# Attention followed by a gated mixture of experts: reordering the preparation of the leftover expert at the end of the kernel

## The chip, the core and the metric

The kernel runs on one core of a Trainium2 chip. The metric is the device time of one execution in microseconds; the median of three runs before the change is 463.12 us (463.02 to 463.18). All other times come from one execution taken by the hardware profiler, whose span from the first to the last instruction is 462.4 us; its mean granted TensorE clock is 0.997 of full speed.

## What is computed

Multi-query attention (8 batches, 16 heads, 384 tokens, head size 64, one key and value head per batch) gives `x` with 3072 rows of 1024. Each row then goes through one of 16 experts (4 groups of 4), chosen by two argmax gates and weighted by both softmax values:

```python
attn = softmax(q @ k.T / 8) @ v              # per batch and head
x = attn.transpose(0, 2, 1, 3).reshape(3072, 1024)
g_idx = argmax(x @ w_group)                  # 4 groups
e_idx = argmax(x @ w_expert[g_idx])          # 4 experts in the group
out[tok] = g_w * e_w * (relu(x[tok] @ w1[g, e]) @ w2[g, e])
```

With these inputs nearly all rows of a batch choose the same expert. So the kernel computes, for each batch, the one most frequent expert over all its 384 rows, with a weight of zero for rows that chose another. What is left over is handled apart: the kernel keeps a table of the (batch, expert) pairs that are also needed. One such pair is computed on the fast path for up to 32 tokens ("the leftover pair"); if more pairs or more tokens turn up, or the scores are too large for an exponential without a maximum, a branch ("the rare case") at the end does the work slowly. In this draw the branch is not taken.

## The kernel before

**Stages.** A loop over 24 steps (8 batches of 3 blocks of 128 tokens) computes scores, exponentials and values for attention; beside it the expert work runs in *units*. The unit list of a batch has 14 entries: 8 "h" units (line 407: eight 128x384 matmuls into one PSUM buffer, evicted by ScalarE on line 408) and 6 "y" units (line 417: eight 128x512 matmuls, evicted on line 419, or by `merge` on line 449, and stored on lines 439 and 441). Numbers like y(1,0) below mean block of tokens 1, left half of the columns. `fill(n)` (line 476) emits the next n units of whichever batch comes next. There is no scheduler: each engine's order is the order of the program, written out by hand, and `fill` is what puts TensorE work between the short, dependent steps of the other engines.

**The end.** After the loop only units remain, and the leftover pair has to be found, gathered, computed and added. Before the change the order from line 639 on is:

1. three y units of batch 6, then the last values of attention (`values`, `join`, `invert`, `weigh`). `weigh` makes `xbf`, the bf16 input of the experts, and stores it to `x_bf` in DRAM (line 303).
2. two y units, the gate matmuls of the last two blocks (line 312), the gate's softmax on VectorE (`gate_math`), `bound_a`, then two units (the last y of batch 6 and h0 of batch 7), `counts(None, last)` (line 340, PE; line 342, ACT; then six VectorE operations of `gate_c`) and `bound_b` (line 512, two transposes, then four VectorE operations), which tests whether the scores were small enough.
3. the load of `xe` (line 656): all rows of the batch that holds the leftover pair, read back from `x_bf`. Its batch number is a register, so it must wait for the store of line 303. Then a chain of short VectorE operations from `gi` (line 659) to `mb` (line 667).
4. one unit (h1), the prefix counts `pr` (lines 672 and 673), eight VectorE operations to `pick`, the 0/1 matrix which sends token to slot; two units (h2, h3), `pg` (line 691), the transpose of `of_last` (line 698), and VectorE operations up to `rarei`, the flag of the rare case (line 710).
5. one unit (h4); then three times eight transposes `pb` of `xe` (line 717) with one unit after each (h5, h6, h7); the gather `px` (line 726), y(0,0), the hidden layer `ph` (735), y(0,1), its transpose `phT` (741), y(1,0), the output `py` (749), y(1,1), `spread`.
6. `spread` (line 453) turns the leftover rows that belong to the last 128 tokens of the output into a tile `yl`: eight matmul records on line 458 and two ScalarE copies on line 461. The leftover rows elsewhere are scattered to DRAM by one indirect DMA on GpSimd (line 755). y(2,0), then the register load of `rarei` on all five engines (line 757), then y(2,1) in two parts of 256 columns; all three are evicted by `merge`, which adds `yl`.
7. the branch on `rare` (line 809; the profile puts its instructions on line 810), and the end of the kernel (line 901).

**Buffers.** `side` tiles (`hps`, `yps`, `pr`, `pg`, `pb` ...) share three PSUM buffers in rotation, so a PE step waits for the reader of the tile three allocations before. `ps_m` has one more buffer. **Queues.** The DMA issues of SyncE (lines 303, 439, 441, 656) run in program order, and one that waits holds those behind it. Leftover `w1` and `w2` are loaded by GpSimd (lines 145, 574); `w2` starts when the last y unit of batch 6 has freed its buffer.

Of the kernel before, what the change touches and what calls it, by code (L numbers as in the profile page):

```python
# [9 lines left out]
FP32 = mybir.dt.float32  # L10
BF16 = mybir.dt.bfloat16
I32 = mybir.dt.int32
U32 = mybir.dt.uint32
P = 128
ACTF = mybir.ActivationFunctionType
OP = mybir.AluOpType
AX = mybir.AxisListType.X
# [4 lines left out]
def kernel(  # L22
# [406 lines left out]
    def first_units(b):  # L429
        rows = {}  # L430

        def place(st, cs):
            if cs.start == 0:
                rows[st] = pool.tile([P, Dm], FP32, tag="y", bufs=3, name="y")
            return rows[st][:, cs]

        def store(st, cs, y):
            if closes(st):
                nc.sync.dma_start(out=outv[b, :, st, cs], in_=y)
            elif cs.stop == Dm:  # L440
                nc.sync.dma_start(out=outv[b, :, st, :], in_=rows[st][:])

        def closes(st):
            return b == B - 1 and st == ST - 1

        def merge(st, cs, ps, y):
            if not closes(st):
                return False
            nc.vector.scalar_tensor_tensor(out=y, in0=ps[:], scalar=gsel[b][:, st:st + 1], in1=leftover["y"][:, cs], op0=OP.mult, op1=OP.add)
            return True  # L450
        return moe_units(wts[b][0], wts[b][1], xbf[b], lambda: gsel[b], place, store, merge, lambda st, nh: 2 if closes(st) and nh == 1 else 1)

    def spread():
        lo = [ps_m.tile([P, 2, CW], FP32, tag="o", name="lo"), side([P, 2, CW], FP32, "lo2")]
        for i in range(2):
            for c in (i, 2 + i):
                r = slice(CAP * c, CAP * c + CAP)
                nc.tensor.matmul(out=lo[c // 2][:, c % 2, 0:QW], lhsT=leftover["spread"][r, :], rhs=leftover["yc"][r, :], start=True, stop=True, tile_position=(CAP * c, 0))
        t = pool.tile([P, Dm], FP32, tag="pt", bufs=9, name="yl")
        for i in range(2):  # L460
            nc.scalar.copy(out=t[:, i * CW:(i + 1) * CW].rearrange("p (c n) -> p c n", c=2), in_=lo[i][:, :, 0:QW])
        leftover["y"] = t

    NP = B * ST
# [11 lines left out]
    def fill(n):  # L476
        while n > 0:
# [10 lines left out]
            if ran[0] == (FO + 2 * ST) * (B - 1):  # L488
                leftover_w2()

    def gates(b):
        if b == 0:
            choose_a(0, gate_a(0, 0, 1))
            return
        ps = gate_a(b, 0, ST)
        choose_a(b, ps)
        gate_logits(b - 1, ps, 1, ST)
        gate_math(b - 1)
# [76 lines left out]
        leftover["w2"] = w2  # L575
    for p in range(NP):
        b, st = divmod(p, ST)
        jobs = [lambda: gates(0), lambda: None, lambda: counts(0, None)] if p == 2 else []
        if p == 0 or p == ST or (st == 1 and 1 < b < B - 1):
            load_q(b + 1)  # L580
        for j in range(3):
            scores(p, j)
            if p == 0 and j == 0:
                turn_q(1, lambda h: q_raw[0][:, 1, h], [nc.vector.tensor_copy])
        if p == 0:
            stats_k(0)
            prep_k(1)
        elif p == ST:
            prep_q(p + 1)
        if jobs:  # L590
            jobs.pop(0)()
        for j in (1, 2):
            pre_add(p, j)
        for j in range(KB):
            if p > 0:
                values(p - 1, j)
            if j == 2 and p > 0:
                join(p - 1)
            if j + 3 < KB:
                scores(p, j + 3)  # L600
            if 0 < j < 4:
                pre_add(p, j + 2)
            if j == 2 and p > 0:
                invert(p - 1)
            if j == 3:
                stats_q(p)
                if p == 1:
                    turn_q(2, lambda h: q_raw[0][:, 2, h], [nc.scalar.copy])
                elif p == 2:
                    turn_q(3, lambda h: q_nat[0][:, h], [nc.scalar.copy])  # L610
            if jobs:
                jobs.pop(0)()
            if p == ST + 1 and j == 0:
                fill(3)
            if st == 1 and 0 < b < B - 1 and j == 0:
                load_k(b + 1)
            if 0 < j < 5:
                some_q(1 if p <= ST + 1 else 2)
            if st == 1 and b + 1 < B and j == KB - 1:
                load_v(b + 1)  # L620
        assert not jobs
        if p > 0:
            weigh(p - 1)
        fold_keys(p)
        if st == 2 and b + 1 < B:
            stats_k(b + 1)
        if p in PHASES:
            n = PHASES[p]
            steps = {}
            prep_q(p + 1)  # L630
            if b == B - 1:
                steps = {1: lambda: gates(b), 2: lambda: counts(b, None), 3: lambda: (counts(None, b - 1), early_pair())}
            else:
                steps = {2: lambda: gates(b), 4: lambda: (counts(b, b - 1), turns(p))}
            for i in range(n):
                fill(1)
                if i in steps:
                    steps[i]()
    fill(3)
    for j in range(KB):  # L640
        if j == 2:
            join(NP - 1)
# [1 line left out]
    invert(NP - 1)  # L644
    weigh(NP - 1)
    last = B - 1
    fill(2)
    gate_logits(last, gate_a(last, 1, ST), 1, ST)
    gate_math(last)
    bound_a()  # L650
    fill(2)
    counts(None, last)
    bound_b()

    xe = pool.tile([P, KO, S], BF16, tag="qraw", bufs=2, name="xe")
    nc.sync.dma_start(out=xe[:].rearrange("p k s -> p (k s)"), in_=xb_dram[bass.ds(leftover["b"], 1)].rearrange("a p k -> (a p) k"))
    gi = leftover["gi"]
    ge = gi[:, :, 0]
    nc.vector.tensor_copy(out=ge, in_=gate_all[:, bass.ds(leftover["reg"], 1), :].rearrange("p a s -> p (a s)"))
# [5 lines left out]
    nc.vector.tensor_copy(out=mb[:, 1, 1:2], in_=m[:, 0:1])  # L665
    nc.vector.tensor_add(out=mb[:, 1, 2:3], in0=m[:, 0:1], in1=m[:, 1:2])
    nc.vector.tensor_add(out=mb[:, 1, 3:4], in0=mb[:, 1, 2:3], in1=m[:, 2:3])
    nfl = pool.tile([P, 1], FP32, tag="nfl", bufs=1, name="nfl")
    nc.vector.reduce_sum(out=nfl[:], in_=extra[:], axis=AX)
    fill(1)  # L670
    pr = side([P, CW], FP32, "pr")
    nc.tensor.matmul(out=pr[:, 0:4], lhsT=prefix[:], rhs=mb[:, 0, :], start=True, stop=False)
    nc.tensor.matmul(out=pr[:, 0:4], lhsT=ones_bf[:], rhs=mb[:, 1, :], start=False, stop=True)
    rk = pool.tile([P, 4], FP32, tag="rk", bufs=1, name="rk")
    nc.vector.tensor_copy(out=rk[:], in_=pr[:, 0:4])

    small = pool.tile([P, 2], FP32, tag="small", bufs=1, name="small")
    nc.vector.tensor_scalar(out=small[:, 0:1], in0=leftover["known"][:], scalar1=1.0, scalar2=None, op0=OP.is_ge)
    nc.vector.scalar_tensor_tensor(out=small[:, 0:1], in0=rk[:, 3:4], scalar=float(CAP), in1=small[:, 0:1], op0=OP.is_le, op1=OP.mult)
# [1 line left out]
    pick = pool.tile([P, ST, P], FP32, tag="part", bufs=1, name="pick")  # L681
    for st in range(ST):
        nc.vector.tensor_scalar(out=pick[:, st, :], in0=rank_of[:], scalar1=rk[:, st:st + 1], scalar2=m[:, st:st + 1], op0=OP.is_equal, op1=OP.mult)
    pick_bf = pool.tile([P, ST, CAP], BF16, tag="kT", name="pick_bf")
    nc.vector.tensor_copy(out=pick_bf[:], in_=pick[:, :, 0:CAP])
    of_last = pool.tile([P, 2, P], FP32, tag="presum", bufs=1, name="of_last")
    nc.vector.tensor_scalar(out=of_last[:, 0, :], in0=pick[:, ST - 1, :], scalar1=leftover["final"][:, 0:1], scalar2=None, op0=OP.mult)
    fill(2)
    pg = side([P, CW], FP32, "pg")
    for st in range(ST):  # L690
        nc.tensor.matmul(out=pg[:, 0:2], lhsT=pick[:, st, :], rhs=gi[:, st, :], start=(st == 0), stop=(st == ST - 1))
    gc = pool.tile([P, 2], FP32, tag="gc", bufs=1, name="gc")
    nc.vector.tensor_copy(out=gc[:, 0:1], in_=pg[:, 0:1])
    nc.vector.tensor_scalar(out=gc[:, 1:2], in0=pg[:, 1:2], scalar1=4.0, scalar2=quarter[:, 0:1], op0=OP.mult, op1=OP.add)
    rows = pool.tile([P, 1], U32, tag="rows", bufs=1, name="rows")
    nc.vector.tensor_copy(out=rows[:], in_=gc[:, 1:2])

    nc.tensor.transpose(out=pg[:, P:2 * P], in_=of_last[:, 0, :], identity=ident[:])
    nc.vector.tensor_copy(out=of_last[:, 1, :], in_=pg[:, P:2 * P])
    leftover["spread"] = of_last[:, 1, :]  # L700

    nc.vector.tensor_sub(out=small[:, 1:2], in0=nfl[:], in1=small[:, 0:1])
    nex = pool.tile([1, 1], I32, tag="nex", bufs=1, name="nex")
    nc.vector.tensor_copy(out=nex[:], in_=small[0:1, 1:2])
    raref = pool.tile([1, 2], FP32, tag="raref", bufs=1, name="raref")
    nc.vector.tensor_scalar(out=raref[:, 0:1], in0=small[0:1, 1:2], scalar1=0.0, scalar2=None, op0=OP.is_gt)
    nc.vector.tensor_scalar(out=raref[:, 1:2], in0=bound["okf"][:], scalar1=-1.0, scalar2=1.0, op0=OP.mult, op1=OP.add)
    nc.vector.tensor_add(out=raref[:, 0:1], in0=raref[:, 0:1], in1=raref[:, 1:2])
    rarei = pool.tile([1, 1], I32, tag="rarei", bufs=1, name="rarei")
    nc.vector.tensor_copy(out=rarei[:], in_=raref[:, 0:1])  # L710
    fill(1)

    xtok = []
    for st in range(ST):
        pb = side([P, Dm], BF16, "pb")
# [3 lines left out]
        nc.vector.tensor_copy(out=xt[:], in_=pb[:])  # L719
        xtok.append(xt)  # L720
        fill(1)
    assert len(units) == 2 * ST
    px = side([P, KO, CAP], FP32, "px")
    for ko in range(KO):
        for st in range(ST):
# [24 lines left out]
    yc = pool.tile([P, QW], FP32, tag="pt", bufs=9, name="yc")  # L750
    nc.scalar.activation(out=yc[:], in_=py[:], func=ACTF.Copy, scale=gc[:, 0:1])
    leftover["yc"] = yc
    fill(1)
    spread()
    nc.gpsimd.indirect_dma_start(out=out4[0:4 * (N - P)], out_offset=bass.IndirectOffsetOnAxis(ap=rows[:], axis=0), in_=yc[:], in_offset=None, bounds_check=4 * (N - P) - 1, oob_is_err=False)  # L755
    fill(1)
    rare = nc.values_load(rarei[0:1, 0:1], min_val=0, max_val=2, skip_runtime_bounds_check_because="a sum of two comparisons")  # L757
    fill(1)

    def load_pair(pair):  # L760
        e_reg, b_reg = parts_of(pair)
# [144 lines left out]
```

## Time and profile before

| | |
|---|---|
| time | 463.12 us |
| span of the profiled execution | 462.4 us |
| PE busy | 449.4 us, 97% |
| DVE, ACT busy | 308.8 us (67%), 241.6 us (52%) |
| h unit, eight matmuls back to back | a start every 0.16 us |
| last matmul ends | 454.6 us |
| end of the kernel after that | 7.8 us |

PE is the TensorE matmul, PEld its weight load, DVE is VectorE, ACT ScalarE, POOL GpSimd, SP SyncE; a q after a name means the sequencer of that engine. A line such as `start, duration, engine line operation out<-in` is one run of like instructions; `[0.39 <-ACT hT L408]` says that the engine stood idle for 0.39 us before it and what ended that. A matmul's printed duration (0.326 us for 384 columns) is about twice the interval between two starts (0.163 us)[...]. So a printed idle time understates by some 0.16 us how much later the work behind it runs.

### The profile page before, as it was taken

What the parts mean: (1) busy time and instruction counts of PE and PEld (TensorE: products, weight loads), DVE (VectorE), ACT (ScalarE), POOL (GpSimd) and SP (SyncE); (2) the same over time, 40 slices, a digit from 0 to 9 for tenths busy, and PEclk for the clock granted to TensorE, in tenths of its full rate; (3) what the DMA queues carried; (4) which work ended last, traced back from release to release, by engine and by line L of the source; (5) the groups of instructions that cost most, each with busy time, mean ns of one, the idle gap of its engine ahead of it and who ended that gap; (6) DMA issues with size and microseconds to landing.
All of it is one profiled execution on the core that took longest, in us unless ns stands there. A gap on an engine that the chain in (4) does not pass through costs nothing. (4 is left out here: it accounts for less than half of the span.)

```text
span 462.4 us, 10190 instructions
## 1 busy us (share of the span) xinstructions
PE 449.4 (97%) x4196; PEld 200.4 (43%) x4208; DVE 308.8 (67%) x489; ACT 241.6 (52%) x345; POOL 60.4 (13%) x83
## 2 busy tenths in 40 slices
PE   8999999999999999999999999999999999999893
PEld 6334445333643345433543336433453335434551
DVE  4899965499708985199834997089852999554511
ACT  2966643676347743566436763477435664532231
POOL 1004003000210103000030002101030001501000
PEclk9999999999999999999999999999999999999998
DMA  8688997997599296993979566992969910999952
GB/s 164 92 141 116 217 215 106 262 191 150 95 197 251 53 205 93 246 197 89 152 121 272 109 139 106 216 243 44 199 100 252 188 69 2 162 217 268 270 134 104
DMA packets 152454, 74.55 MB, mean 161 GB/s; under 512 B 120256, under 2 KB 138944, under 8 KB 152400
## 3 DMA queue, kind: packets, MB, share of 16 engines
q0 software_dynamic: 28416, 37.81, 48.0%
q1 hardware_dynamic: 122656, 35.68, 33.0%
q8 instruction: 35, 0.57, 0.5%
q10 hardware_dynamic: 1328, 0.33, 0.4%
q14 instruction: 19, 0.16, 0.1%
HBM read 92.62 MB, written 19.01 MB: 241 GB/s over the span
## 5 line engine op out<-in xcount | busy, mean ns | idle before, releaser
L253 ACT ACTIVATE pt<-s 128x1024 f32<-128x1024 f32 x144 | 142.1, 1026 | 71.9 <-PE s L251 71.2
L251 PE MATMUL s<-qT,kT 64*64 64x512 f32 x1152 | 142.4, 594 | 0.3 <-ACT qT L229 0.2
L290 PE MATMUL o<-pt,v 64*64 64x512 f32 x1152 | 141.1, 590 | 0.0
L261 DVE TENSOR_TENSOR presum<-presum,pt 128x1024 f32<-128x1024 f32 x96 | 116.6, 1215 | 15.2 <-ACT pt L253 9.8
L407 PE MATMUL hps<-xbf,w 128*128 128x384 bf16 x512 | 87.3, 326 | 0.4 <-ACT hT L408 0.4
L417 PE MATMUL yps<-w,hT 128*128 128x512 bf16 (+1 forms) x380 | 84.6, 375 | 0.6
L259 DVE TENSOR_TENSOR presum<-pt 128x1024 f32<-128x1024 f32 x24 | 29.4, 1223 | 76.8 <-ACT pt L253 75.4
L290 PEld LDWEIGHTS o<-pt,v 64*64 64x64 f32 x1152 | 43.4, 133 | 76.8 <-issue 73.0
L251 PEld LDWEIGHTS s<-qT,kT 64*64 64x64 f32 x1152 | 40.8, 133 | 66.8 <-issue 60.0
L407 PEld LDWEIGHTS <-w 128*128 128x128 bf16 x512 | 48.1, 98 | 38.1 <-issue 7.3
L301 POOL CAST xbf<-xT 128x1024 bf16<-128x1024 f32 x24 | 25.0, 1041 | 302.7 <-DVE xT L300 302.7
L419 ACT ACTIVATE y<-yps,gsel 128x512 f32<-128x512 f32 x46 | 31.6, 687 | 56.9 <-PE yps L417 55.3
L408 ACT ACTIVATE hT<-hps 128x384 bf16<-128x384 f32 x64 | 31.2, 488 | 55.6 <-PE hps L407 52.4
L417 PEld LDWEIGHTS <-hT 128*128 128x128 bf16 x392 | 37.7, 98 | 44.6 <-issue 2.4
L145 POOL DMA_DIRECT2D w<-in_moe_w_dram x36 | 24.8, 707 | 58.1 <-DVE gsel L395 37.7
L300 DVE TENSOR_TENSOR xT<-o,rinv 128x1024 f32<-128x1024 f32 x24 | 29.2, 1215 | 2.5 <-PE o L290 2.5
L280 DVE STREAM_TRANSPOSE rinv<-rc 128x1024 f32<-128x1024 f32 x24 | 29.9, 1245 | 0.8
L265 DVE TRANSPOSE_TENSOR_REDUCE fold<-presum 128x32 f32<-128x1024 f32 x24 | 29.6, 1232 | 0.0
L243 DVE STREAM_TRANSPOSE qT<-qraw 128x1024 f32<-128x1024 f32 x20 | 23.6, 1202 | 0.0
L209 ACT ACTIVATE qraw<-qraw 128x1024 f32<-128x1024 f32 x21 | 22.0, 1049 | 0.0
L273 PEld LDWEIGHTS sm<-fold,sel 64*64 64x64 f32 x192 | 7.3, 133 | 13.3 <-issue 13.3
L312 PE MATMUL gps<-xT,gw 128*32 128x96 f32 (+2 forms) x576 | 12.6, 239 | 0.0
(152 smaller groups left out, 152.9 us busy)
## 6 DMA issues: line engine op xcount, KB each, us to landing
w<-in_moe_w_dram POOLq DMA_DIRECT2D x36, 512.0 KB, 11.3
w<-in_moe_w_dram POOLq DMA_DIRECT2D x9, 2048.0 KB, 25.9
out_dram<-y SPq DMA_DIRECT2D x23, 512.0 KB, 6.9
qraw<-in_q_dram SPq DMA_DIRECT2D x56, 192.0 KB, 3.6
x_bf<-xbf SPq DMA_DIRECT2D x8, 768.0 KB, 4.0
v<-in_v_dram SPq DMA_DIRECT2D x16, 96.0 KB, 3.1
k<-in_k_dram SPq DMA_DIRECT2D x28, 48.0 KB, 2.7
qn<-in_q_dram SPq DMA_DIRECT2D x4, 256.0 KB, 5.2
```

Source lines behind the costliest of these rows:

```text
L251: nc.tensor.matmul(out=ps[64 * c:64 * c + 64, a, :], lhsT=kT[b][r, j * D:(j + 1) * D], rhs=qT[p][r, c * CW:(c + 1) * CW], start=True, stop ...
L253: nc.scalar.activation(out=t[:], in_=ps[:], func=ACTF.Exp, scale=scale)
L259: nc.vector.tensor_add(out=presum[p][:], in0=pt[p, 0][:], in1=pt[p, 1][:])
L261: nc.vector.tensor_add(out=presum[p][:], in0=presum[p][:], in1=pt[p, j][:])
L265: nc.vector.tensor_reduce(out=fold[p][:], in_=presum[p][:].rearrange("p a (n i) -> p (a n) i", i=32), axis=AX, op=OP.add, apply_transpose= ...
L280: nc.vector.transpose(out=t[:].rearrange("p (b i) -> p b i", i=32), in_=rc[:].rearrange("p c b -> p (c b)").unsqueeze(2).to_broadcast([P, ...
L290: nc.tensor.matmul(out=o_ps[p][64 * a:64 * a + 64, c, :], lhsT=v_sb[b][r, j, :], rhs=pt[p, j][r, a, :], start=(j == 0), stop=(j == KB - 1))
L300: nc.vector.tensor_mul(out=xT[b][:, :, ts], in0=o_ps[p][:].rearrange("p c (h n) -> p (c h) n", n=P), in1=rinv[p][:].rearrange("p (h n) -> ...
L407: nc.tensor.matmul(out=ps[:, 0:S], lhsT=w1[:, ko, fc * P:(fc + 1) * P], rhs=xb[:, ko, :], start=(ko == 0), stop=(ko == KO - 1))
L408: nc.scalar.activation(out=state["h"][:, fc, :], in_=ps[:, 0:S], func=ACTF.Relu)
L417: nc.tensor.matmul(out=ps[:], lhsT=state["h"][:, fo, st * P:(st + 1) * P], rhs=w2[:, fo, cs], start=(fo == 0), stop=(fo == FO - 1))
L419: nc.scalar.activation(out=y, in_=ps[:], func=ACTF.Copy, scale=gs_of()[:, st:st + 1])
```

## The change

The change is about steps 2 to 7. Its purpose is that no step of the leftover's preparation has TensorE waiting:

- `bound_a` and `bound_b` move ahead of the last values, with two units and one unit after them.
- The load of `xe` is put directly after `weigh`, ahead of the last two stores of batch 6, which were in front of it on SyncE.
- `counts(None, last)` and the sum `nfl` move from ahead of the `gi` chain to behind `pick`: the preparation needs only `gate_math`, not the final counts.
- There are three units ahead of `pr` (before: one), two ahead of `pg`, three ahead of the first `pb` (before: one). The transposes of `of_last` come directly after `pg`, ahead of the VectorE reads of `pg`.
- The units that this takes are missing later: `px` has y(0,1) ahead of it, `ph` y(1,0), `phT` y(1,1), `py` y(2,0).
- `spread` moves into y(2,1), between its two parts. y(2,0) is evicted by ScalarE as an ordinary unit; its leftover part is added in place by VectorE (`tensor_add`), and then stored. `yl` is half as wide, so one ScalarE copy of 512 elements goes.
- The three operations for `rarei` (before: four) and its register load come after the last unit.

```diff
         def store(st, cs, y):
             if closes(st):
-                nc.sync.dma_start(out=outv[b, :, st, cs], in_=y)
+                if cs.start == 0:
+                    leftover["row"] = y
+                else:
+                    nc.sync.dma_start(out=outv[b, :, st, cs], in_=y)
...
         def merge(st, cs, ps, y):
-            if not closes(st):
+            if not closes(st) or cs.start == 0:
                 return False
-            nc.vector.scalar_tensor_tensor(out=y, in0=ps[:], scalar=gsel[b][:, st:st + 1], in1=leftover["y"][:, cs], op0=OP.mult, op1=OP.add)
+            if cs.start == CW:
+                spread()
+            nc.vector.scalar_tensor_tensor(out=y, in0=ps[:], scalar=gsel[b][:, st:st + 1], in1=leftover["y"][:, cs.start - CW:cs.stop - CW], op0=OP.mult, op1=OP.add)
             return True
...
-        t = pool.tile([P, Dm], FP32, tag="pt", bufs=9, name="yl")
-        for i in range(2):
-            nc.scalar.copy(out=t[:, i * CW:(i + 1) * CW].rearrange("p (c n) -> p c n", c=2), in_=lo[i][:, :, 0:QW])
+        row = leftover["row"]
+        nc.vector.tensor_add(out=row.rearrange("p (c n) -> p c n", c=2), in0=row.rearrange("p (c n) -> p c n", c=2), in1=lo[0][:, :, 0:QW])
+        nc.sync.dma_start(out=outv[B - 1, :, ST - 1, 0:CW], in_=row)
+        t = pool.tile([P, CW], FP32, tag="pt", bufs=9, name="yl")
+        nc.scalar.copy(out=t[:].rearrange("p (c n) -> p c n", c=2), in_=lo[1][:, :, 0:QW])
...
+    def rest_of_gates(b):
+        gate_logits(b, gate_a(b, 1, ST), 1, ST)
+        gate_math(b)
...
-    fill(3)
+    bound_a()
+    fill(2)
+    bound_b()
+    fill(1)
     for j in range(KB):
...
     last = B - 1
-    fill(2)
-    gate_logits(last, gate_a(last, 1, ST), 1, ST)
-    gate_math(last)
-    bound_a()
-    fill(2)
-    counts(None, last)
-    bound_b()
-
     xe = pool.tile([P, KO, S], BF16, tag="qraw", bufs=2, name="xe")
     nc.sync.dma_start(out=xe[:].rearrange("p k s -> p (k s)"), in_=xb_dram[bass.ds(leftover["b"], 1)].rearrange("a p k -> (a p) k"))
+    fill(2)
+    rest_of_gates(last)
     gi = leftover["gi"]
...
-    nfl = pool.tile([P, 1], FP32, tag="nfl", bufs=1, name="nfl")
-    nc.vector.reduce_sum(out=nfl[:], in_=extra[:], axis=AX)
-    fill(1)
+    fill(3)
     pr = side([P, CW], FP32, "pr")
...
-    fill(2)
+    fill(1)
+    counts(None, last)
+    nfl = pool.tile([P, 1], FP32, tag="nfl", bufs=1, name="nfl")
+    nc.vector.reduce_sum(out=nfl[:], in_=extra[:], axis=AX)
+    fill(1)
     pg = side([P, CW], FP32, "pg")
     for st in range(ST):
         nc.tensor.matmul(out=pg[:, 0:2], lhsT=pick[:, st, :], rhs=gi[:, st, :], start=(st == 0), stop=(st == ST - 1))
+    nc.tensor.transpose(out=pg[:, P:2 * P], in_=of_last[:, 0, :], identity=ident[:])
     gc = pool.tile([P, 2], FP32, tag="gc", bufs=1, name="gc")
...
-    nc.tensor.transpose(out=pg[:, P:2 * P], in_=of_last[:, 0, :], identity=ident[:])
...
-    nc.vector.tensor_copy(out=rarei[:], in_=raref[:, 0:1])
-    fill(1)
-
+    fill(3)
     xtok = []
...
     leftover["yc"] = yc
-    fill(1)
-    spread()
     nc.gpsimd.indirect_dma_start(out=out4[0:4 * (N - P)], out_offset=bass.IndirectOffsetOnAxis(ap=rows[:], axis=0), in_=yc[:], in_offset=None, bounds_check=4 * (N - P) - 1, oob_is_err=False)
     fill(1)
...
+    nc.vector.tensor_add(out=rarei[:], in0=raref[:, 0:1], in1=raref[:, 1:2])
     rare = nc.values_load(rarei[0:1, 0:1], min_val=0, max_val=2, skip_runtime_bounds_check_because="a sum of two comparisons")
-    fill(1)
```

More of the change, by code (lines that the diff above doesn't have):

```diff
@@ L435, in place, with closes @@
             return rows[st][:, cs]
+        def closes(st):
+            return b == B - 1 and st == ST - 1
         def store(st, cs, y):
             if closes(st):
-                nc.sync.dma_start(out=outv[b, :, st, cs], in_=y)
+                if cs.start == 0:
+                    leftover["row"] = y
+                else:
+                    nc.sync.dma_start(out=outv[b, :, st, cs], in_=y)
             elif cs.stop == Dm:
                 nc.sync.dma_start(out=outv[b, :, st, :], in_=rows[st][:])
-        def closes(st):
-            return b == B - 1 and st == ST - 1
         def merge(st, cs, ps, y):
-            if not closes(st):
+            if not closes(st) or cs.start == 0:
                 return False
-            nc.vector.scalar_tensor_tensor(out=y, in0=ps[:], scalar=gsel[b][:, st:st + 1], in1=leftover["y"][:, cs], op0=OP.mult, op1=OP.add)
+            if cs.start == CW:
+                spread()
+            nc.vector.scalar_tensor_tensor(out=y, in0=ps[:], scalar=gsel[b][:, st:st + 1], in1=leftover["y"][:, cs.start - CW:cs.stop - CW], op0=OP.mult, op1=OP.add)
             return True
@@ L489, in fill @@
                 leftover_w2()
+    def rest_of_gates(b):
+        gate_logits(b, gate_a(b, 1, ST), 1, ST)
+        gate_math(b)
     def gates(b):
-        if b == 0:
-            choose_a(0, gate_a(0, 0, 1))
-            return
         ps = gate_a(b, 0, ST)
@@ L577 @@
         b, st = divmod(p, ST)
-        jobs = [lambda: gates(0), lambda: None, lambda: counts(0, None)] if p == 2 else []
+        jobs = [lambda: choose_a(0, gate_a(0, 0, 1)), lambda: None, lambda: counts(0, None)] if p == 2 else []
         if p == 0 or p == ST or (st == 1 and 1 < b < B - 1):
@@ L683 @@
         nc.vector.tensor_scalar(out=pick[:, st, :], in0=rank_of[:], scalar1=rk[:, st:st + 1], scalar2=m[:, st:st + 1], op0=OP.is_equal, op1=OP.mult)
+    of_last = pool.tile([P, 2, P], FP32, tag="presum", bufs=1, name="of_last")
+    nc.vector.tensor_scalar(out=of_last[:, 0, :], in0=pick[:, ST - 1, :], scalar1=leftover["final"][:, 0:1], scalar2=None, op0=OP.mult)
     pick_bf = pool.tile([P, ST, CAP], BF16, tag="kT", name="pick_bf")
     nc.vector.tensor_copy(out=pick_bf[:], in_=pick[:, :, 0:CAP])
-    of_last = pool.tile([P, 2, P], FP32, tag="presum", bufs=1, name="of_last")
-    nc.vector.tensor_scalar(out=of_last[:, 0, :], in0=pick[:, ST - 1, :], scalar1=leftover["final"][:, 0:1], scalar2=None, op0=OP.mult)
-    fill(2)
+    fill(1)
[3 more added lines that the diff above has]
+    fill(1)
     pg = side([P, CW], FP32, "pg")
@@ L704 @@
     nc.vector.tensor_copy(out=nex[:], in_=small[0:1, 1:2])
[L705 to L709, printed above, removed]
-    nc.vector.tensor_copy(out=rarei[:], in_=raref[:, 0:1])
-    fill(1)
+    fill(3)
     xtok = []
@@ L721 @@
         fill(1)
-    assert len(units) == 2 * ST
     px = side([P, KO, CAP], FP32, "px")
@@ L752 @@
     leftover["yc"] = yc
-    fill(1)
-    spread()
     nc.gpsimd.indirect_dma_start(out=out4[0:4 * (N - P)], out_offset=bass.IndirectOffsetOnAxis(ap=rows[:], axis=0), in_=yc[:], in_offset=None, bounds_check=4 * (N - P) - 1, oob_is_err=False)
     fill(1)
+    assert ran[0] == UNITS * B
+    raref = pool.tile([1, 2], FP32, tag="raref", bufs=1, name="raref")
+    nc.vector.tensor_scalar(out=raref[:, 0:1], in0=small[0:1, 1:2], scalar1=0.0, scalar2=None, op0=OP.is_gt)
+    nc.vector.tensor_scalar(out=raref[:, 1:2], in0=bound["okf"][:], scalar1=-1.0, scalar2=1.0, op0=OP.mult, op1=OP.add)
+    rarei = pool.tile([1, 1], I32, tag="rarei", bufs=1, name="rarei")
+    nc.vector.tensor_add(out=rarei[:], in0=raref[:, 0:1], in1=raref[:, 1:2])
     rare = nc.values_load(rarei[0:1, 0:1], min_val=0, max_val=2, skip_runtime_bounds_check_because="a sum of two comparisons")
-    fill(1)
     def load_pair(pair):
```

## The prediction

> **What bounds the kernel now.** I read the profile's summary first, then busy time by stretch, the waits of the stretch that stands out, TensorE's timeline there, the input it waits for last, and the end.
>
> ```profile
> span 462.4 us, 10190 instructions
> PE 449.4 (97%) x4196; PEld 200.4 (43%) x4208; DVE 308.8 (67%) x489; ACT 241.6 (52%) x345; POOL 60.4 (13%) x83
> ```
>
> TensorE is the bound: its order and its gaps set the time. Busy time in four stretches at the end (us in the stretch, then busy per engine, clock, DMA share, GB/s):
>
> ```profile
> 398.00:424.00 26.00, 25.84 (x258) 10.46 (x254) 13.99 (x19) 10.13 (x14) 3.44 (x5) 1.00 1.17 217
> 424.00:435.15 11.15, 8.21 (x54) 4.83 (x51) 6.58 (x42) 3.23 (x7) 0.88 (x1) 1.00 1.10 312
> 435.15:454.60 19.45, 19.28 (x199) 11.38 (x202) 4.03 (x7) 6.12 (x11) 0.00 (x0) 1.00 0.66 153
> 454.60:462.44 7.84, 0.00 (x0) 0.00 (x0) 0.48 (x1) 0.00 (x0) 1.09 (x1) 0.80 0.25 83
> ```
>
> All idle time is between 424.0 and 435.15 (2.94 us) and after the last matmul (7.8 us). Where it lies, from TensorE's timeline:
>
> ```profile
> 425.99 1.46 PE L407 MATMUL hps<-xbf,w 128*128 128x384 bf16 x8 [0.39 <-ACT hT L408]
> 428.65 0.18 PE L672 MATMUL pr<-mb,prefix 128*128 128x4 bf16 x1 [1.20 <-DVE mb L664]
> 428.97 0.17 PE L673 MATMUL pr<-mb,ones_bf 128*128 128x4 bf16 x1
> ...
> 432.69 0.33 PE L698 MATMUL pg<-ident,of_last 128*128 128x128 f32 x1 [0.37 <-DVE gc L694]
> 432.85 1.47 PE L407 MATMUL hps<-xbf,w 128*128 128x384 bf16 x8
> 435.15 0.62 PE L717 MATMUL pb<-ident_bf,xe 128*128 128x128 bf16 x8 [0.83 <-DMA xe<-x_bf]
> ```
>
> Four named gaps, and 0.14 us between L672 and L673 (428.83 to 428.97, `mb`'s last operation). Each costs about 0.16 us more than printed, since matmuls otherwise start while the last drains: 0.39 + 1.20 + 0.14 + 0.37 + 0.83 = 2.93, plus 5 x 0.16 = 3.7 us. The last one is a transfer, `xe`:
>
> ```profile
> L656 SPq EVENT_SEMAPHORE  x1: 2649/2649/2649, 425.3 to 425.3; - x1
> L656 SPq DMA_DIRECT2D xe<-x_bf x1: 365/365/365, 428.1 to 428.1; - x1
> ...
> DMA to landing us min/median/max: 7.0/7.0/7.0
> ```
>
> SyncE stood at L656 from 425.3 and was let go 2.65 us later, at 427.97. The waits of SyncE name the store of `x_bf` (issued 420.1, landing 7.8 us later). So `xe` leaves at 428.07 because of that store, not because of its place in the program, and lands at 435.1.
>
> At the end, by source line (events of the branch, and of the scatter):
>
> ```profile
> L810 SPq EVENT_SEMAPHORE  x9: 17/17/17, 456.1 to 459.5; - x9
> L810 PEldq COMPARE_BRANCH  x2: 95/2216/4338, 452.3 to 454.9; - x2
> L755 POOLq EVENT_SEMAPHORE  x5: 43/43/28746, 424.9 to 454.0; - x5
> L901 POOLq DRAIN  x3: 46/103/870, 460.7 to 462.2; - x3
> ```
>
> Two ends nearly tie: SyncE's last store (issued 455.49) has landed by 459.5, and the scatter, started at 454.88, by 459.6 (4.7 us). GpSimd's drain of 0.87 us and the closing barrier follow. TensorE's second branch took 4.34 us, from 454.93 to 459.27, and is hidden by these.
>
> **The Trainium skill.** "DMA: Bandwidth & Descriptors", Issuing engines are not separate DMA queues: transfers of all issuers interleave on the same 16 DMA engines. The trace agrees: the store of `x_bf` and the load of `xe`, 768 KB each, take 7.8 and 7.0 us while GpSimd's weights stream, against 4.0 us, the median of the eight `x_bf` stores in the profile's table of DMA issues. So I don't shorten `xe` for being issued elsewhere. "Runtime: NRT & Kernel Launch", Instruction fetch mechanics: a taken branch whose target is outside the fetched window waits for a fetch by DMA. That fits the 4.34 us; the trace also has 2.7 us on ACT (452.3 to its drain at 455.0).
>
> **Part by part.**
>
> *bound_a and bound_b ahead of the values.* The VectorE operations run at about 410, where DVE shows idle until `invert` (4.37 us before 414.22): nothing. The two transposes (L512, 0.38 us less the overlap of 0.16: 0.2 to 0.25) only move: nothing in sum, but values, `weigh` and the store of `x_bf` run 0.25 us later. The 0.39 us wait at h1 goes: `cps` and `pq` no longer take two of the three PSUM buffers between h0 and h1. With overlap, minus 0.55.
>
> *counts after pick, three units before pr.* Before, `mb` was ready at 428.9, since behind `gate_math` (ends 424.5) DVE waited for `cnt` and did `gate_c` and `bound_b`. Now the seven operations (0.9 us) follow `gate_math`: `mb` at 424.5 + 0.25 + 0.9 = 425.7. `pr` comes after y, h0 and h1: 422.15 + 0.25 + 1.73 + 2 x 1.30 = 426.7, so it doesn't wait: minus (1.20 + 0.14 + 2 x 0.16) = 1.65. Behind it, DVE needs 1.6 us (rk 429.17 to pick 430.75) and 0.5 for `of_last` and `pick_bf`: ready at 428.7 to 429.0. `pg` comes after h2, `cps`, h3: 426.7 + 0.2 + 2.6 + 0.1 = 429.6. No wait. The counts (six operations, 1.1 us, and `nfl` 0.28) run on DVE to about 430.4, just as `pg` ends; the reads of `pg` queued behind them (`gc`, `rows`, `of_last`) take 1 us, and what waits for them is `yc` and `spread`, over 15 us later: nothing.
>
> *Transpose before the reads of pg.* It waited for `gc`; now it follows: minus 0.37 + 0.16 = 0.53.
>
> *Three units before pb; xe earlier in the program.* Without its wait TensorE would reach `pb` at 435.15 - 3.7 + 2 x 1.30 = 434.0. But `xe` waits for `x_bf`, which is issued 0.25 us later; SyncE was already waiting. So it leaves at 428.3. What is gained is only that two stores of 512 KB no longer lie ahead of it in the queue. Its 7.0 us is unknown now: the least is that median of 4.0 us, the most is the 7.8 us of `x_bf`, which had nothing of SyncE ahead of it and was no faster. I take 7.0: landing 435.3, `pb` at 435.4, a wait of 1.4 us. The stores pushed back have no reader near: the next user of their buffers is y(1,0) of batch 7, past 441.
>
> *From pb to the last matmul.* Before: 454.59 - 435.15 = 19.44 us with no gap. Two h units went ahead, minus 2.6: 16.8 us. Each chain step keeps a y unit (1.73 us) in front, against `xc` 0.5, `hg` 0.45, `hc` 0.35 us. `yc` needs 0.55 us after `py` and now has one part of y(2,1) (0.87 us) ahead of its reader: no wait. `py` runs at 435.4 + 16.8 - 3.5 = 448.7, and `w2` (424.88 + 20.8 = 445.7) is there. Last matmul: 452.2 instead of 454.59, minus 2.35.
>
> *The tail.* `spread` in the middle of y(2,1) puts the addition (0.75 us, by the 128x512 merge) ahead of two merges of 0.48 on DVE: 0.3 us later than before relative to the last matmul. But SyncE issued its last store only 0.9 us after the last matmul, because a register load of 0.56 us (L757) and three issues of 0.34 were in the way; with the load gone it issues at the same distance. The scatter waited until 453.8, when the store of y(1,1) (issued 451.12) had landed; now that store goes out a unit earlier relative to `yc`, so the scatter starts up to 1 us earlier. SyncE alone is then the end: minus 0.2 to 0.6. Against it, `rarei` exists 1.2 us after the last matmul, the register load takes 0.34 to 0.69 on each engine, and TensorE's second branch starts at 2.2 instead of 0.3 us after the last matmul: with 4.34 us it ends at 6.6, where SyncE's drain was at 6.4. A tie, so I take minus 0.25 for the tail, with plus 1.5 if the fetch is slower there.
>
> Sum: -0.55 - 1.65 - 0.53 from three waits, +0.4 for `xe` (1.4 for 1.0) = -2.35, tail -0.25: 463.12 - 2.6 = 460.5.
>
> **The rivals.**
>
> 1. *xe still late* (the forecast, 0.52): 460.5. For it: `xe`'s issue hangs on `x_bf`, and both loaded transfers took 7 to 8 us.
> 2. *xe in time* (0.28): with the stores out of its way, or `x_bf` landing 1 us sooner, it is there by 434.1: 463.12 - 3.7 - 0.25 = 459.2. Against it: weights keep the DMA share above 1.0 until 444.
> 3. *The tail takes back part* (0.13): the branch on all engines now follows the last addition, and its fetch meets the last stores. Plus 1.5 us: 462.0.
> 4. *Slower* (0.07): `xe` takes as long as the slowest store (9.5 us) and lands at 437.8; last matmul 454.7; with the longer tail, +1.3: 464.5. Against it: those 9.5 us were a store behind `x_bf`, while `xe` is first in its queue.
>
> **How the numbers follow.** The likeliest is 460.5. The range from 459.0 to 462.2 takes in the first two, most of the third, and `xe` between 4.0 and 7.8 us. Faster by over 0.2% means below 462.2: 0.52 + 0.28 + about 0.06 of the third = 0.86. The rest of the third and a weak form of the fourth give 0.08 for no difference, and 0.06 remains for slower.
>
> **What would show it.** L672, L673 and L698 without idle time in front, and h1 not waiting for L408. `pb` (L717) still waiting for `xe`, by 1 to 1.5 us; `xe` issued near 428.3, not at 421. Last matmul near 452.2, and 7.6 us from there to the end. The forecast is wrong if `pb` doesn't wait (459.2), if `x_bf` lands elsewhere than 428, if a new wait appears at `pr` or `px`, or if the last drain is TensorE's and not SyncE's.

## The result and the profile after

| | before | after |
|---|---|---|
| time, median of 6 runs | 463.24 us | 461.01 us |
| span of the profiled execution | 462.4 us | 459.6 us |
| last matmul ends | 454.59 us | 452.33 us |
| from there to the end | 7.85 us | 7.30 us |

The ratio is 0.9948, with a 95% interval from 0.9935 to 0.9960: 2.2 us faster by the medians and 2.4 by the ratio, between 1.9 and 3.0. The forecast was 460.5 us.

The profile's summary of the changed kernel:

```profile
span 459.6 us, 10200 instructions
PE 449.4 (98%) x4208; PEld 199.8 (43%) x4208; DVE 308.4 (67%) x488; ACT 242.0 (53%) x345; POOL 60.5 (13%) x83
```

TensorE's busy time is the same, so what went is idle time. Busy time in the four stretches, cut at the same events as before (start of h0, 0.3 us later now; first `pb`; last matmul):

```profile
398.30:424.30 26.00, 26.00 (x259) 10.48 (x252) 14.98 (x25) 9.91 (x14) 3.23 (x4) 1.00 1.18 219
424.30:435.49 11.19, 9.95 (x68) 6.14 (x65) 5.11 (x32) 4.21 (x9) 0.89 (x1) 1.00 1.12 274
435.49:452.33 16.84, 16.84 (x186) 9.80 (x186) 3.67 (x7) 5.38 (x9) 0.93 (x1) 1.00 0.72 197
452.33:459.60 7.27, 0.00 (x0) 0.00 (x0) 0.86 (x5) 0.00 (x0) 0.17 (x1) 0.67 0.28 93
```

The second stretch is as long as before (11.19 against 11.15 us), but TensorE is now busy for 9.95 us of it instead of 8.21. The third is 16.84 us instead of 19.45: the two h units that are now ahead of `pb`. TensorE's timeline where its waits were:

```profile
424.18 2.76 PE L407 MATMUL hps<-xbf,w 128*128 128x384 bf16 x16
426.77 0.17 PE L675 MATMUL pr<-mb,prefix 128*128 128x4 bf16 x1
426.80 0.16 PE L676 MATMUL pr<-mb,ones_bf 128*128 128x4 bf16 x1
...
429.45 0.73 PE L697 MATMUL pg<-gi,pick 128*128 128x2 f32 x6
430.04 0.31 PE L698 MATMUL pg<-ident,of_last 128*128 128x128 f32 x1
430.18 4.06 PE L407 MATMUL hps<-xbf,w 128*128 128x384 bf16 x24
435.49 0.62 PE L715 MATMUL pb<-ident_bf,xe 128*128 128x128 bf16 x8 [1.24 <-DMA xe<-x_bf]
```

None of the waits at h1, `pr` or the transpose is left; the one at `pb` has grown from 0.83 to 1.24 us. Its transfer, by the line that issues it:

```profile
L659 SPq EVENT_SEMAPHORE  x1: 7069/7069/7069, 420.9 to 420.9; - x1
L659 SPq DMA_DIRECT2D xe<-x_bf x1: 365/365/365, 428.1 to 428.1; - x1
...
DMA to landing us min/median/max: 7.4/7.4/7.4
```

SyncE stands at the load 4.4 us earlier than before (420.9 instead of 425.3), and is let go at the same moment, when `x_bf` has landed. The end of the kernel, by its closing line (each engine closes with an instruction called drain), before and then after, and below them the branch's line (durations in ns as least, median and most, then the first and last start in us):

```profile
L901 SPq DRAIN  x3: 7/7/13, 460.9 to 461.9; - x3
L901 PEldq DRAIN  x2: 8/40/73, 459.3 to 461.9; - x2
```

```profile
L901 SPq DRAIN  x3: 7/7/13, 457.3 to 459.1; - x3
L901 PEldq DRAIN  x2: 7/40/73, 458.7 to 459.1; - x2
```

```profile
L810 PEldq COMPARE_BRANCH  x2: 95/1986/3876, 454.3 to 454.8; - x2
```

Now TensorE's drain (458.7) is the last one; before, it was over by 459.4 while GpSimd's drain began at 460.7 and took 0.87 us, and SyncE's began at 460.9. TensorE's branch starts at 454.8, 2.46 us after the last matmul instead of 0.34. In all ten traces the kernel ends 0.8 to 0.9 us after the last engine has drained.

### The profile page after: what moved, and what is told of

The parts are those of the page before. It is cut to its first block, busy times and chain, and to the rows that moved or that the text cites. A ratio compares the mean times of both kernels' runs of the same rounds, so it can differ in the third digit from the quotient of the medians.

```text
span 459.6 us, 10200 instructions
## 1 busy us (share of the span) xinstructions
PE 449.4 (98%) x4208; PEld 199.8 (43%) x4208; DVE 308.4 (67%) x488; ACT 242.0 (53%) x345; POOL 60.5 (13%) x83
## 4 chain that ended last, share of the span: by engine, by line
PE 89%; DMA 4%; issue 2%; DVE 1%; POOL 0%; ACT 0%; ACTq 0%; SPq 0%; POOLq 0%
PE s L251 28%; PE o L290 25%; PE hps L407 16%; PE yps L417 16%; PE gps L312 2%; DMA x_bf<-xbf 2%; DMA xe<-x_bf 2%; DMA qn<-in_q_dram 1%; PE qps L228 1%; POOL xbf L301 0%; DVE presum L261 0%; PE sm L273 0%; PE pb L715 0%; DVE rinv L280 0%; DVE xT L300 0%
## 5 line engine op out<-in xcount | busy, mean ns | idle before, releaser
L417 PE MATMUL yps<-w,hT 128*128 128x512 bf16 (+1 forms) x392 | 85.7, 375 | 0.0
L371 ACT ACTIVATE ex<-dl 128x60 f32<-128x60 f32 x8 | 2.0, 253 | 20.1 <-DVE dl L369 20.1
```

What stands on the lines that cost most here:

```text
L417: nc.tensor.matmul(out=ps[:], lhsT=state["h"][:, fo, st * P:(st + 1) * P], rhs=w2[:, fo, cs], start=(fo == 0), stop=(fo == FO - 1))
```

## The experiments

Two questions were open. Is `xe` late because of the traffic, because of its place in the queue, or by its nature? And what does the late flag of the rare case do to the end? All runs in one table; "late" and "early" say where the flag's register load stands (after or ahead of the last unit). The waits are as printed; drains are given from the last matmul on; "stores" is the median time from issue to landing of the last two stores, and "tail" the time from the last matmul to the end.

| kernel | ratio to before (95%) | time, us | wait at `pb`, us | last matmul, us | stores, us | drain SyncE / TensorE, us | tail, us |
|---|---|---|---|---|---|---|---|
| before (early) | 1 | 463.24 | 0.83 | 454.59 | 3.9 | 6.4 / 4.7 | 7.85 |
| changed (late) | 0.9948 (0.9935 to 0.9960) | 461.01 | 1.24 | 452.33 | 2.5 | 5.1 / 6.4 | 7.30 |
| changed again, c1 (late) | 0.9944 (0.9930 to 0.9958) | 461.33 | 1.16 | 452.50 | 2.3 | 4.9 / 5.9 | 6.82 |
| b1 before, flag late | 0.9982 (0.9976 to 0.9989) | 462.91 | 0.83 | 454.64 | 2.2 | 4.2 / 5.8 | 6.65 |
| e1 changed, flag early | 0.9940 (0.9927 to 0.9954) | 460.91 | 1.06 | 452.51 | 3.6 | 5.8 / 4.3 | 6.66 |
| e2 a unit more (late) | 0.9918 (0.9902 to 0.9934) | 459.99 | none | 451.38 | 2.3 | 4.8 / 6.1 | 6.99 |
| e3 `xe` behind the stores (late) | 0.9926 (0.9912 to 0.9939) | 460.69 | 0.68 | 452.43 | 2.3 | 4.9 / 5.9 | 6.76 |
| e4 no leftover weights (late) | 0.9912 (0.9899 to 0.9926) | 459.80 | none | 451.46 | 2.5 | 5.0 / 6.3 | 7.18 |
| e5 a unit more, flag early | 0.9918 (0.9905 to 0.9932) | 459.94 | none | 451.54 | 3.8 | 6.1 / 4.6 | 6.90 |
| e6 as e5, load behind the last unit | 0.9916 (0.9902 to 0.9929) | 459.77 | none | 450.77 | 4.1 | 6.7 / 5.0 | 7.50 |

The times of b1, e1, e2 and e4 stand beside a median of 463.87 us for the kernel before, those of c1, e3, e5 and e6 beside 463.84 us; so compare the ratios.

### e4: take the traffic away

```diff
-        w1 = wpool.tile([P, KO, F], BF16, tag="w1", name="w1")
-        load_w1(w1, leftover["e"])
-        leftover["w1"] = w1
+        leftover["w1"] = wts[B - 1][0]
...
-        leftover["w2"] = w2
+        leftover["w2"] = wts[B - 1][1]
```

> The changed kernel with the 4 MB of the leftover expert's own weights left out: it takes batch 7's w1 and w2 instead, so the up to 32 leftover rows are computed with another expert's weights. All else stays. Theory (the store of x_bf and the load of xe are slow, 7.6 and 7.4 us, because the weights stream over the same DMA engines): both land in about 4 us, xe leaves near 424.5 and is there by 429, TensorE doesn't wait at the transposes, last matmul 450.9, time 459.6. Rival (a store followed by a dependent load of this size takes this long by itself): 7 us each, wait and time unchanged at 461.0.

Busy time by stretch in this kernel, for the stretch in which `x_bf` is stored and `xe` loaded; the last but one number is the share of the DMA engines:

```profile
418.00:424.00 6.00, 6.00 (x93) 2.92 (x86) 2.03 (x6) 1.37 (x2) 1.04 (x1) 1.00 0.36 138
424.00:428.00 4.00, 4.00 (x27) 2.30 (x25) 2.16 (x16) 1.90 (x4) 0.00 (x0) 1.00 0.32 49
```

and in the changed kernel:

```profile
418.00:424.00 6.00, 6.00 (x88) 3.05 (x87) 2.33 (x7) 1.63 (x3) 1.04 (x1) 1.00 1.26 216
424.00:428.00 4.00, 4.00 (x28) 2.39 (x27) 2.35 (x16) 1.67 (x3) 0.89 (x1) 1.00 1.11 288
```

The two transfers in this kernel (the landing times are those of `x_bf`, their median, and `xe`):

```profile
L303 SPq DMA_DIRECT2D x_bf<-xbf x1: 332/332/332, 420.9 to 420.9; - x1
L655 SPq DMA_DIRECT2D xe<-x_bf x1: 364/364/364, 425.6 to 425.6; - x1
...
DMA to landing us min/median/max: 4.5/4.9/5.2
```

With the share down from above 1.1 to about 0.35, `x_bf` lands in 4.5 us (7.6 in the changed kernel) and `xe` in 5.2 (7.4). `xe` leaves at 425.6, and TensorE reaches the transposes at 434.6 with no wait. So the two transfers are late because the weights stream beside them: the theory holds, though neither came down to the 4 us expected, and the last matmul is 451.46 and not 450.9 (this execution is 0.5 us later already when it issues `x_bf`, at 420.9 and not 420.4).

### e3: undo the place of xe in the queue

```diff
-    xe = pool.tile([P, KO, S], BF16, tag="qraw", bufs=2, name="xe")
-    nc.sync.dma_start(out=xe[:].rearrange("p k s -> p (k s)"), in_=xb_dram[bass.ds(leftover["b"], 1)].rearrange("a p k -> (a p) k"))
     fill(2)
     rest_of_gates(last)
...
-    fill(3)
+    fill(1)
+    xe = pool.tile([P, KO, S], BF16, tag="qraw", bufs=2, name="xe")
+    nc.sync.dma_start(out=xe[:].rearrange("p k s -> p (k s)"), in_=xb_dram[bass.ds(leftover["b"], 1)].rearrange("a p k -> (a p) k"))
+    fill(2)
```

> The changed kernel with the load of xe put back behind the two 512 KB stores of batch 6 on SyncE (after mb and one unit). Theory of the prediction (xe is held by the landing of x_bf, and its place in SyncE's queue matters little): x_bf lands at 428.0, xe leaves at 428.1 and lands at 435.1 to 435.5, TensorE's wait is 1.0 to 1.4 us, the time that of the changed kernel within 0.3. Rival (two stores of 512 KB ahead of it in the queue, at the 280 to 340 GB/s of this stretch, cost it up to 3.5 us, and the old 7.0 us contained them): xe lands near 438, last matmul 455, time up by 2 to 3 us.

```profile
435.58 0.62 PE L716 MATMUL pb<-ident_bf,xe 128*128 128x128 bf16 x8 [0.68 <-DMA xe<-x_bf]
```

```profile
L673 SPq DMA_DIRECT2D xe<-x_bf x1: 364/364/364, 428.7 to 428.7; - x1
...
DMA to landing us min/median/max: 6.8/6.8/6.8
```

`xe` leaves at 428.7 behind both stores and lands 6.8 us later, at 435.5, as in the changed kernel. The rival (landing near 438) falls. Putting `xe` ahead in the queue gains nothing, as forecast. It may even cost something: all five runs of e3 (460.19 to 460.79 us) lie below all five of c1 (460.82 to 461.80) on the same chip, 0.6 us by the medians, where 0.3 at most was expected. In its trace `xe` is in the air for 6.8 us against 7.3 in c1, but `x_bf` is issued 0.4 us later in this execution, and the last matmuls are 0.07 us apart. Whether the shorter flight is the cause stays open.

### e2: hide the wait

```diff
-    fill(3)
+    fill(4)
     xtok = []
...
         xtok.append(xt)
-        fill(1)
+        fill(1 if st else 0)
```

> The changed kernel with one more h unit ahead of the first transposes of xe (four instead of three) and none between the first and the second block of transposes. Theory: TensorE waits 1.4 us for xe, a transfer whose time doesn't depend on TensorE's order, so a unit of 1.30 us moved ahead hides that much: the wait falls to 0.1 us, the last matmul from 452.3 to 451.0, the time to about 459.7. Rival: xe is late because it shares the engines' DMA with w2, which starts with the last y unit of batch 6; then nothing in this kernel moves it either, and the gain is the same, but if the second block of transposes now waits for the copy of the first, or px for the third copy, 0.5 to 0.7 us of it are given back: 460.3.

```profile
432.75 2.93 PE L407 MATMUL hps<-xbf,w 128*128 128x384 bf16 x17
435.58 1.07 PE L715 MATMUL pb<-ident_bf,xe 128*128 128x128 bf16 x16
...
447.72 1.06 PE L746 MATMUL py<-w,hc 128*32 128x256 bf16 x32 [0.18 <-DMA w<-in_moe_w_dram]
```

The wait at `pb` is gone, though `xe` comes no earlier (435.6), and neither the second block of transposes nor `px` waits. The last matmul moves by 0.95 us (1.3 us expected): some of the rest shows as a new wait of 0.18 us at `py`, where `w2` has become what arrives last. It was 22.3 us in the air here and landed at 447.6, against 20.5 us and 445.6 in the changed kernel; why it took longer is not shown. A further unit moved ahead could meet that. The time is 1.2 to 1.4 us below the changed kernel by the ratios.

### b1 and e1: the rare flag alone, and without it

b1 adds to the kernel before what follows; e1 undoes the same in the changed kernel, and has the three operations after `nex` and the load ahead of the last unit.

```diff
-    raref = pool.tile([1, 2], FP32, tag="raref", bufs=1, name="raref")
...
-    nc.vector.tensor_copy(out=rarei[:], in_=raref[:, 0:1])
     fill(1)
...
-    rare = nc.values_load(rarei[0:1, 0:1], min_val=0, max_val=2, skip_runtime_bounds_check_because="a sum of two comparisons")
     fill(1)
+    raref = pool.tile([1, 2], FP32, tag="raref", bufs=1, name="raref")
...
+    nc.vector.tensor_add(out=rarei[:], in0=raref[:, 0:1], in1=raref[:, 1:2])
+    rare = nc.values_load(rarei[0:1, 0:1], min_val=0, max_val=2, skip_runtime_bounds_check_because="a sum of two comparisons")
```

> The kernel before with one part of the change alone: the three operations for rarei and its register load come after the last unit. Theory A (the fetch of TensorE's branch takes about 4 us whenever it starts): TensorE's drain comes 6.4 us after the last matmul, level with SyncE's (6.4) and ahead of GpSimd's (7.06), which waits for the scatter: the time stays at 463.2 within 0.3. Rival B (fetches collide with stores): the last stores and the scatter land about 1 us sooner, as no branch is taken while they run, and the time falls by 0.5 to 0.8 us.

> The changed kernel with one part undone: rarei is computed after nex and its register load stands ahead of the last unit, as before the change. Theory A (the late flag makes TensorE's branch the last to finish: its drain at 458.72 in the changed kernel, 6.4 us after the last matmul, while SyncE's drain is at 457.39): TensorE's branch starts 0.3 instead of 2.4 us after the last matmul, its drain comes some 1.9 us sooner, SyncE becomes the end, and the time falls by 1.3 us to about 459.7. Rival B (what the late flag costs on the branch it saves elsewhere: before the change the instruction fetches of the early branches ran while the last stores did, and the last store took 3.84 us instead of 2.5): the last store lands about 1.3 us later again, SyncE's drain goes to 458.7, and the time stays at 461.0 within 0.3. The stores' time from issue to landing tells which.

DMA issues in the last 9 us of the kernel before: what, KB each, us to landing.

```profile
out_dram<-y SPq DMA_DIRECT2D x1, 256.0 KB, 2.3
out_dram<-y SPq DMA_DIRECT2D x2, 128.0 KB, 3.9
out_dram<-yc,rows POOLq DMA_INDIRECT x1, 4.7
```

and of b1:

```profile
out_dram<-y SPq DMA_DIRECT2D x1, 256.0 KB, 2.4
out_dram<-y SPq DMA_DIRECT2D x2, 128.0 KB, 2.2
out_dram<-yc,rows POOLq DMA_INDIRECT x1, 2.5
```

In b1 the scatter starts at the same time (454.9) and lands in 2.5 us instead of 4.7; the last stores land in 2.2 instead of 3.9. Nothing but the flag differs (its operations, one fewer, its register load, and the branch that follows the load). So the early load and branch cost these transfers about 2 us: rival B holds here. The time falls by 0.8 us (0.5 to 1.1), and TensorE's drain becomes the last.

e1 gives the other side. The line of the last two stores (445) in e1, and the closing line:

```profile
DMA to landing us min/median/max: 3.5/3.6/3.7
```

```profile
L901 SPq DRAIN  x3: 7/7/13, 458.3 to 458.6; - x3
L901 PEldq DRAIN  x2: 8/40/73, 456.8 to 458.7; - x2
```

The stores are slow again (3.6 us against 2.5). SyncE is now the end, with GpSimd, whose drain is over at the same moment (458.3). TensorE's drain (456.8) is out of the way by 1.9 us, as theory A said. The two nearly cancel: ratio 0.9940 against 0.9944 and 0.9948 of the changed kernel. Both theories name a real cost, and neither gives the whole time.

e1 is also the reordering without the flag: it brings 0.60% alone, and the flag alone brought 0.18% in the old order. Together they bring 0.52 to 0.56%, so the flag's gain does not add: in the old order it shortened the landing of the scatter, on which the end hung (GpSimd's drain). In the new order the scatter starts before the last matmul: with the early flag of e1 it takes 4.3 us, but has landed (456.3) before the last store (456.8).

### c1, e5 and e6: the flag in the better order

> The changed kernel itself, on the same chip as the three beside it, since the differences looked for are below 1 us. All theories: ratio to the kernel before 0.995, span 459.6, tail after the last matmul 7.3 us, TensorE's drain last.

c1 is the changed kernel once more. It shows how much the tail moves by itself: 6.82 instead of 7.30 us. TensorE's register load took 0.65 us here and 0.97 there, its branch 3.68 and 3.88.

e5 is e2 with the flag as in e1; e6 is e2 with only the three operations moved up:

```diff
     nc.vector.tensor_copy(out=nex[:], in_=small[0:1, 1:2])
+    raref = pool.tile([1, 2], FP32, tag="raref", bufs=1, name="raref")
...
+    nc.vector.tensor_add(out=rarei[:], in0=raref[:, 0:1], in1=raref[:, 1:2])
     fill(4)
```

> The changed kernel with one more unit ahead of the first transposes (as in the run with four) and the rare flag and its register load back ahead of the last unit. If the early flag is better in this order (TensorE's branch is the end with the late one: 6.1 to 6.4 us after the last matmul): tail 6.6 instead of 7.0 to 7.3, time 0.4 to 0.6 us below the run with four units and the late flag, that is 1.8 us below the changed kernel. If the early flag's fetches delay the last stores by as much as TensorE gains: the same time as with the late flag, 1.4 us below the changed kernel.

> As the run before, but only the flag is computed early; the register load stays after the last unit, so each engine loads when its own work is done and none waits for VectorE's last additions. Theory (start of TensorE's branch counts, its 3.9 us are fixed): the load starts about 0.1 instead of 0.9 us after the last matmul, the branch at 1.2 instead of 2.1 to 2.5, TensorE's drain at 5.2, SyncE's at 5.0 to 5.8, tail 6.2 to 6.6. Rival (fetches started while the stores of the last 128 tokens are under way delay them): the stores land 1 us later than with the late flag (SyncE's drain at 5.8 instead of 4.8) and the tail is 6.7 or more.

In e6, the line of the last two stores and the closing line:

```profile
DMA to landing us min/median/max: 4.1/4.1/4.2
```

```profile
L901 SPq DRAIN  x3: 7/7/13, 457.4 to 457.7; - x3
L901 PEldq DRAIN  x2: 8/40/73, 455.8 to 457.8; - x2
```

and TensorE's register load and branch:

```profile
L758 PEldq TENSOR_LOAD <-rarei x1: 483/483/483, 449.1 to 449.1; - x1
```

```profile
L810 PEldq COMPARE_BRANCH  x2: 87/2300/4512, 449.7 to 451.2; - x2
```

e6 didn't come out as its theory had it: with the flag computed early, TensorE's load starts 1.7 us before the last matmul ends, though it stands behind the last unit in the program, and the branch 0.4 us after it (0.1 and 1.2 us after it were expected). So e6 is another kernel with an early branch, and no run separates the flag's register load from the branch.

In e5 and e6 the stores land in 3.8 and 4.1 us, and SyncE's drain comes 6.1 and 6.7 us after the last matmul (4.8 in e2); TensorE's is at 4.6 and 5.0 (6.1 in e2). The ratios are 0.9918, 0.9918 and 0.9916 for e2, e5 and e6. So here, too, an early flag gives with one hand and takes with the other; the rival held in both. The last matmul of e6 is 0.8 us sooner than that of e5 (0.5 us of it is there already when `x_bf` is issued, and `py` doesn't wait for `w2`), and its tail is 0.6 us longer. In all four kernels with an early register load or flag the last stores took 3.6 to 4.1 us, and in all six with a late one 2.2 to 2.5 us. In the traces, a fetch of 16 KB on an instruction queue, 1.0 to 1.9 us long, falls between the packets of the stores in the former (it starts 1.5 to 2.1 us after the last matmul) and after the last of their data in the latter (2.9 to 3.5 us after it). That this fetch is what holds the stores up fits the times, but was not tried by itself.

e2, e5 and e6 are faster than both kernels, by 0.82 to 0.84% against the kernel before; among themselves they are equal.

## Why the prediction was right

The forecast (460.5 us, rival 1) named the waits that would go, the one that would stay, and the time of the last matmul.

- **h1, `pr`, the transpose.** Forecast: none of these waits left, 2.7 us saved. Measured: none is left, and `mb` is ready at 425.74 (forecast 425.7). `pr` was forecast at 426.7 (it starts at 426.77), `pg` at 429.6 (429.45).
- **Bounds ahead of the values, 0.25 us later.** The store of `x_bf` went from 420.1 to 420.4: 0.3 us.
- **`xe` stays late.** Forecast: issue at 428.3 whatever its place in the program, 7.0 us to landing, `pb` at 435.4. Measured: 428.1, 7.4 us, 435.49. e3 shows that the place ahead of the stores gains nothing, e4 that the traffic of the weights is what costs. This agrees with the Trainium skill, "DMA: Bandwidth & Descriptors", Issuing engines are not separate DMA queues, by which transfers of all issuers interleave on the same 16 DMA engines: SyncE's two transfers took 7.6 and 7.4 us beside GpSimd's weights, 4.5 and 5.2 without them.
- **From `pb` on.** Forecast 16.8 us without a gap; measured 16.84. Last matmul forecast at 452.2, measured 452.33.
- **The tail.** Forecast a tie between SyncE (6.4 us after the last matmul) and TensorE's branch (6.6), 7.6 us in all. Measured: TensorE 6.39, SyncE 5.06, and 7.30 and 6.82 (c1) in all. Here the mechanism was wrong in part: of the two ends that were to tie, only TensorE's was there. The prediction counted "the last drain is TensorE's and not SyncE's" among the signs against itself, and that is what came. It left the last store at its old 3.8 us, and it took 2.5, because the flag's load and branch now come later (b1). The register load, taken from before as 0.34 to 0.69 us, took 0.64 to 0.97 (0.57 to 0.66 in c1). That TensorE's end is so near the forecast is partly luck: its branch started later (2.46 us after the last matmul, not 2.2) and was shorter (3.88 us, not 4.34). The third rival, a tail longer by 1.5 us, had the sign of this interaction wrong: the late branch made room for the stores. The branch took TensorE 3.7 to 3.9 us where it was taken late and 3.9 to 4.5 us where it was taken early, so its end follows its start. That fits the Trainium skill, "Runtime: NRT & Kernel Launch", Instruction fetch mechanics, by which a taken branch to a target outside the fetched window waits for a fetch by DMA; no run shows which fetch TensorE waits for.

The sum was 2.6 us, of which the medians show 2.2 (1.9 to 3.0 by the ratio); the profiled spans differ by 2.8. Of these, 2.26 are the last matmul (forecast 2.35) and 0.55 the tail (forecast 0.25). The tail's part is about the scatter of single executions (0.5 us between two profiles of the same kernel), and the runs don't settle it more closely.

## What to carry to other kernels

A wait for a transfer is not shortened by issuing it earlier in the program if its own input is what holds it: look at what the issuing queue waits for, and move work of the bound engine ahead of the wait instead. When one input has been hidden, look for the next that arrives just in time (here `w2`, 0.18 us). A branch at the end of this kernel held TensorE for about 4 us. Taken ahead of the last unit it made the last stores land later; taken behind it, it became the end itself. In the new order, moving it only traded one for the other.

## What the runs showed of the hardware that was not expected

- With the flag's register load and branch ahead of the last unit instead of behind it, the same scatter took 4.7 instead of 2.5 us, and the same 128 KB stores 3.9 instead of 2.2 (before against b1).
- TensorE's jump over the block that was not taken took 3.7 to 4.5 us in every kernel, and the register load of one 4-byte flag between 0.30 and 0.97 us. On TensorE the same load in the same program took 0.97 us in one execution and 0.65 in another (changed and c1).
